# A matmul's moving operand read in four interleaved quarters instead of column by column

## The chip, the cores and the metric

The kernel runs on one core of one Trainium2 chip. The metric is device time in microseconds (us) for one execution of the program; times of single instructions are given in nanoseconds (ns). A core has TensorE (PE; PEld is its weight load), VectorE (DVE), ScalarE (ACT), GpSimd (POOL) and SyncE (SP), which run on their own and wait for each other by semaphores. SyncE, ScalarE and GpSimd issue the transfers (DMA).

## What is computed

The reference mixes two branches of the same input by a gate. Branch A is a Fourier mix written as four matrix products, branch B a dense layer with a squared ReLU and a second dense layer:

```python
# x: (1, 2048, 1024); dft_hid_*: (1024, 1024); dft_seq_*: (2048, 2048); w1: (1024, 3584); w2: (3584, 1024)
g = sigmoid((x * gate_w).sum(-1, keepdims=True))
a = einsum("bsd,ed->bse", x, dft_hid_re)
b = einsum("bsd,ed->bse", x, dft_hid_im)
y = einsum("ts,bse->bte", dft_seq_re, a) - einsum("ts,bse->bte", dft_seq_im, b)
h = einsum("bsd,df->bsf", x, w1) + b1
h = max(h, 0) ** 2
o = einsum("bsf,fd->bsd", h, w2) + b2
out = g * y + (1 - g) * o
```

All of it is float32.

## The kernel before

**Arithmetic.** Every product of two float32 blocks is made of three matmuls. Each operand is split into `hi` (the value rounded to the matmul's 32-bit type fp32r, ScalarE's `Copy`) and `lo` (the value minus `hi`, a VectorE subtraction), and `hi·hi`, `hi·lo` and `lo·hi` are added up in PSUM. Above that stand two levels of a seven-product scheme for 2x2 blocks (`FACTORS`, `SUMS_L`, `SUMS_R`, L59 to L72): seven products instead of eight, for sums and differences of blocks which VectorE makes (tiles named `sum`, or `raw` where a block is overwritten) or a transfer adds while it lands.

**Stages.** `x_stage` makes a and b of the hidden transform (tiles `ab`), `c_stage` the sequence transform (tiles `y`), two parts of `h_stage` the first dense layer (tiles `h`), and `o_stage` the second one and the mix (tiles `o`). Results between stages lie in DRAM.

**A step.** A block is 128 partitions x 2 x 512 values, 512 KB. A step is one pair of operands: `Group.run` (L534 to L560) issues for each of the up to four rows of 128 weight columns, for each of the two halves `kk`, and for each of the three pairs of `hi` and `lo` one matmul: weights of 128 x 128 (the stationary operand `a`) against 512 columns (the moving operand `b`). So a full step has 24 matmuls, and all 7896 of them have this shape, in any stage. The moving operand is a whole `hi` or `lo` tile, `b[:, kk, :]`: 512 neighbouring float32 of each partition. When a group of steps ends, VectorE or ScalarE takes the PSUM bank (`ps`) up: `ab<-u,ps` is such an addition.

**What each operand is in which stage.** In `x_stage` x is stationary and the transform's matrix (`w4`) is moving; in `c_stage` ab is stationary and the sequence matrix (`ct`) moving; in `h_stage` w1 is stationary and x moving; in `o_stage` w2 is stationary and h moving.

**Order.** The kernel's operations are recorded first (`Op`, `Queue`) and then put in order by `plan` (L1372 to L1521), a model of the machine with a cost per operation: TensorE's matmuls keep their order, each with a due time `MM` (0.2267 us) after the one before it; every other operation is due by the matmul that needs it, and each engine's queue takes what is ready and due first. `emit` (L1524) writes the result out, so an engine's instructions stand in the order that the model found. 55 `SLOTS` of one block each hold all operands; the four pairs of PSUM banks are given out in turn. Before the first step `WARM` = 44 small bf16 matmuls of 128 columns run on a tile of ones.

**Host side.** `kernel` (L1559) only re-lays the inputs with numpy (`laid`) and the output at the end.

Of the kernel before, what the change touches and what calls it, by code (L numbers as in the profile page):

```python
# [15 lines left out]
P = 128  # L16
S, D, F = 2048, 1024, 3584
# [18 lines left out]
MADE = {"T1": 2568, "T3": 11876}  # L36
TWICE_H = (1, 2, 5, 3, 4, 6, 7), (1, 2, 5, 3, 4, 6)

MM, MM_END, FIRST_MM = 0.2267, 0.18, 6.2
VEC, VEC_END, ACT, ACT_END = (0.07, 1.0417e-3), 0.39, (0.09, 0.843e-3, 0.04, 0.095), 0.41  # L40
ADDING = 0.85, 2.1, 2.2
ISSUE, RING, RATE, SEM, LANES = {"sync": 0.36, "scalar": 0.36, "gpsimd": 0.56}, {"sync": (1.8, 1.8), "scalar": (1.8, 1.8), "gpsimd": (1.6, 1.6)}, (420e3, 395e3), 0.06, 8
# [33 lines left out]
def gated_mix_kernel(ctx: ExitStack, tc: tile.TileContext, x4, xn, w4, ct, w1a, w1b, w2, b1, b2, gw, out):  # L76
# [143 lines left out]
    def run(*parts):  # L220

        for _ in zip_longest(*parts):
            pass
# [57 lines left out]
    class Part(Near):  # L281
# [21 lines left out]
        def load(self, engines):  # L303
            if self.lands:
                self.slots = [take("raw", width=self.width)]
                a, b = (b.at if isinstance(b, Kept) else b for b in self.blocks)
                at = self.slots[0][:, :, 0:self.width]
                next(engines).dma_start(at, a)
                nc.gpsimd.dma_start(at, b, accum_op=ADD)
            else:  # L310
                run(self.load_parts(engines))
# [24 lines left out]
        def sum(self):  # L336
            run(self.make_parts())
# [59 lines left out]
    class Operand:  # L397
# [28 lines left out]
        def sum(self):  # L426
            run(self.sum_parts())
# [86 lines left out]
    class Group:  # L514
# [27 lines left out]
        def run(self, st, mv, by_part=False):  # L542
            if not self.ps:
                self.prepare()
            self.at += 1
            ends = self.at % self.k == 0
            mms = [(r, kk, n) for r in range(self.rows) for kk in range(2) for n in range(3)]
            if by_part:
                mms.sort(key=lambda e: (e[1], e[0] // 2, e[2], e[0]) if e[1] == 0 else (e[1], e[2], e[0]))
            for r, kk, n in mms:  # L550
                a, b = ((st.hi, mv.hi), (st.hi, mv.lo), (st.lo, mv.hi))[n]
                nc.tensor.matmul(self.ps[r // self.per][:, r % self.per, :], a[:, kk, r * P:(r + 1) * P],
                                 b[:, kk, :], start=self.at == 1 and kk + n == 0 and not self.onto,
                                 stop=ends and kk == 1 and n == 2,
                                 skip_group_check=bool(self.at > self.k or self.onto))
                if ends and self.per == 1 and kk == 1 and n == 2:
                    self.done[0][0](r // 2, self.ps[r], r % 2)
                elif ends and (r % 2 or r == self.rows - 1) and kk == 1 and n == 2:
                    self.done[self.at // self.k - 1][0](r // 2, self.ps[r // 2])
            if self.at == self.k * len(self.done):  # L560
                banks.extend(self.pools)
# [1031 lines left out]
```

## Time and profile before

| what | value |
|---|---|
| median of 3 runs | 1817.81 us (1817.16 to 1818.1) |
| span of the profiled execution, first to last instruction | 1816.2 us |
| mean granted TensorE clock | 0.999 |
| instructions | 22349 |
| transfers | 562.63 MB, mean 310 GB/s |

The profile shows one execution. For it only the span is known; the times of the runs include what little lies around the span. A group's line gives the source line, engine, operation, the tiles written and read (`lo<-raw,hi` is the subtraction that makes `lo`), the shape and the count; behind the bar its busy time, the mean of one in ns, and the idle time of the engine before such instructions with what ended it. All operations are recorded by a helper and have its line, L1542, so that tiles tell them apart. A matmul's end is modelled, and consecutive matmuls overlap in the profile; their pace is read from start to start.

### The profile page before, as it was taken

The numbers are of one execution on the slowest core, as the hardware profiler recorded it, in microseconds if no ns is written. First come the engines' busy times: TensorE is split into PE (matmuls) and PEld (weight loads), VectorE is DVE, ScalarE is ACT, GpSimd is POOL, SyncE is SP. The second block draws the span as 40 slices with busy tenths as digits, with TensorE's granted clock in tenths as the row PEclk, the third lists the DMA queues.
The fourth block names the chain that finished last, engine by engine and source line by source line (L and its number), as shares of the span: only waits on it lengthen the run. The fifth ranks groups of instructions, "written<-read, shape, count | busy, mean of one in ns | idle before, by whom it ended". The sixth has DMA issues, their size and how long they took to land. (4 is left out here: it accounts for less than half of the span.)

```text
span 1816.2 us, 22349 instructions
## 1 busy us (share of the span) xinstructions
PE 1799.8 (99%) x7940; PEld 1484.5 (82%) x7940; DVE 1711.6 (94%) x1698; ACT 1157.5 (64%) x1274; POOL 284.2 (16%) x415
## 2 busy tenths in 40 slices
PE   9999999999999999999999999999999999999998
PEld 7888878888888888888878888788888888888886
DVE  8999989999999999999779999878998999999997
ACT  6465655774666664666583739967886567575662
POOL 1212112111211100111120201111121021101121
PEclk9999999999999999999999999999999999999999
DMA  9999999999998899989998889999999999979986
GB/s 376 322 393 380 384 331 302 323 273 292 261 354 264 227 306 383 311 216 351 314 371 278 279 299 329 375 381 327 345 362 253 335 241 303 328 192 349 316 218 149
DMA packets 158607, 562.63 MB, mean 310 GB/s; under 512 B 17808, under 2 KB 18080, under 8 KB 158496
## 3 DMA queue, kind: packets, MB, share of 16 engines
q1 hardware_dynamic: 98496, 351.99, 51.4%
q0 software_dynamic: 59712, 208.83, 43.1%
q8 instruction: 62, 1.02, 0.2%
q10 hardware_dynamic: 288, 0.39, 0.1%
q14 instruction: 49, 0.40, 0.1%
HBM read 402.28 MB, written 138.94 MB: 298 GB/s over the span
## 5 line engine op out<-in xcount | busy, mean ns | idle before, releaser
L1542 PE MATMUL ps<-hi 128*128 128x512 f32 x2188 | 852.2, 390 | 6.2 <-DVE h L1542 3.2
L1542 PE MATMUL ps<-hi,lo 128*128 128x512 f32 x2188 | 850.7, 389 | 1.0 <-DVE lo L1542 1.0
L1542 PE MATMUL ps<-lo,hi 128*128 128x512 f32 x2188 | 850.8, 389 | 0.6 <-DVE lo L1542 0.6
L1542 ACT ACTIVATE hi<-raw 128x1024 fp32r<-128x1024 f32 (+2 forms) x452 | 459.1, 1035 | 238.7 <-DVE raw L1542 76.1
L1542 PEld LDWEIGHTS ps<-hi 128*128 128x128 f32 x2188 | 410.6, 188 | 96.9 <-DVE h L1542 5.3
L1542 PEld LDWEIGHTS ps<-hi,lo 128*128 128x128 f32 x2188 | 410.7, 188 | 87.4 <-DVE lo L1542 1.8
L1542 PEld LDWEIGHTS ps<-lo,hi 128*128 128x128 f32 x2188 | 410.5, 188 | 86.4 <-DVE lo L1542 1.5
L1542 DVE TENSOR_TENSOR lo<-raw,hi 128x1024 fp32r<-128x1024 f32 (+2 forms) x385 | 451.5, 1190 | 29.1 <-ACT hi L1542 24.1
L1542 ACT ACTIVATE hi<-sum 128x1024 fp32r<-128x1024 f32 (+1 forms) x248 | 253.8, 1037 | 153.0 <-DVE sum L1542 103.3
L1542 DVE TENSOR_TENSOR lo<-sum,hi 128x1024 fp32r<-128x1024 f32 (+1 forms) x232 | 273.9, 1194 | 14.4 <-ACT hi L1542 5.4
L1542 PE MATMUL ps<-hi,both 128*128 128x512 f32 x888 | 285.0, 389 | 0.0
L1542 DVE TENSOR_TENSOR raw<-raw 128x1024 f32<-128x1024 f32 (+1 forms) x173 | 204.0, 1196 | 5.3 <-DMA raw<-in_w1a 2.6
L1542 PEld LDWEIGHTS ps<-hi,both 128*128 128x128 f32 x888 | 166.6, 188 | 34.7 <-DVE both L1542 0.2
L1542 DVE TENSOR_TENSOR sum<-raw 128x1024 f32<-128x1024 f32 (+2 forms) x180 | 175.6, 985 | 11.1 <-DMA raw<-in_w1a 2.3
L1542 PE MATMUL ps<-lo,both 128*128 128x512 f32 x444 | 172.7, 389 | 0.0
L1542 DVE TENSOR_TENSOR sum<-raw,sum 128x1024 f32<-128x1024 f32 (+2 forms) x135 | 141.3, 1049 | 2.3 <-DMA raw<-in_ct 1.4
L1542 ACT ACTIVATE u<-ps 128x1024 f32<-128x1024 f32 x104 | 101.2, 976 | 34.7 <-PE ps L1542 32.5
L1542 PEld LDWEIGHTS ps<-lo,both 128*128 128x128 f32 x444 | 83.4, 188 | 17.4
L1542 ACT ACTIVATE ps<-u 128x1024 f32<-128x1024 f32 x68 | 67.2, 989 | 35.5 <-DVE u L1542 16.3
L1542 DVE TENSOR_TENSOR u<-u,ps 128x1024 f32<-128x1024 f32 x74 | 86.8, 1184 | 1.9 <-PE ps L1542 1.0
L1542 ACT ACTIVATE both<-sum 128x512 fp32r<-128x512 f32 x74 | 46.3, 625 | 55.5 <-DVE sum L1542 49.2
L1542 DVE TENSOR_TENSOR h<-h,ps 128x1024 f32<-128x1024 f32 (+1 forms) x58 | 61.2, 1067 | 11.6 <-PE ps L1542 11.2
(82 smaller groups left out, 1002.2 us busy)
## 6 DMA issues: line engine op xcount, KB each, us to landing
raw<-in_ct SPq DMA_DIRECT2D x133, 512.0 KB, 8.9
raw<-h SPq DMA_DIRECT2D x104, 512.0 KB, 7.2
raw<-in_w SPq DMA_DIRECT2D x94, 512.0 KB, 9.0
raw<-copy SPq DMA_DIRECT2D x74, 512.0 KB, 7.1
raw<-ab SPq DMA_DIRECT2D x70, 512.0 KB, 10.0
raw<-in_x SPq DMA_DIRECT2D x51, 512.0 KB, 8.7
lo<-lo SPq DMA_DIRECT2D x50, 512.0 KB, 7.0
copy<-raw POOLq DMA_DIRECT2D x46, 512.0 KB, 9.3
```

What stands on the lines that cost most here:

```text
L1542: made = getattr(real[op.engine], op.name)(*(actual(a) for a in op.args), **{k: actual(v) for k, v in op.kwargs.items()})
```

## The change

The matmul's moving operand is read through another access pattern. `b[:, kk, :].rearrange("p (a b) -> p b a", a=4)` takes the 512 columns as 4 quarters of 128 and reads column 0 of each quarter, then column 1 of each quarter, and so on: 128 groups of four columns whose addresses lie 512 bytes apart. The result in PSUM is written in the order of reading, so its columns are permuted: column 4i + q of the result is column 128q + i of the operand. What follows from that is settled in numpy, before and after the program:

- `w4` is laid so that the permuted read of `x_stage` gives the natural order (its result is the stationary operand of the next stage);
- `ct` is laid permuted once, and the read permutes it again; h comes out of `h_stage` permuted once (x is laid as before there) and is permuted again when `o_stage` reads it, so that both branches' results have their columns in the order `twice`;
- the gate's input `xn` is laid in the order `twice`, and the output is put back at the end.

The planner's cost of a matmul is changed with it, from 0.2267 to 0.2157 us.

```diff
-MM, MM_END, FIRST_MM = 0.2267, 0.18, 6.2
+MM, MM_END, FIRST_MM = 0.2157, 0.18, 6.2
...
                 nc.tensor.matmul(self.ps[r // self.per][:, r % self.per, :], a[:, kk, r * P:(r + 1) * P],
-                                 b[:, kk, :], start=self.at == 1 and kk + n == 0 and not self.onto,
+                                 b[:, kk, :].rearrange("p (a b) -> p b a", a=4), start=self.at == 1 and kk + n == 0 and not self.onto,
...
+    seen = np.arange(512).reshape(4, 128).T.ravel()
+    twice = (512 * np.arange(4)[:, None] + seen[seen]).ravel()
     laid = {
...
-        "xn": x.reshape(P, 16, D).transpose(1, 0, 2),
-        "w4": np.stack([a.T.reshape(2, 2, 2, P, 2, 512).transpose(4, 0, 1, 3, 2, 5) for a in w]),
-        "ct": np.stack([a.T.reshape(8, 2, P, 2, 2, 512).transpose(3, 4, 0, 2, 1, 5) for a in c], axis=2),
+        "xn": x[twice].reshape(P, 16, D).transpose(1, 0, 2),
+        "w4": np.stack([a.T.reshape(2, 2, 2, P, 2, 512).transpose(4, 0, 1, 3, 2, 5) for a in w])[..., np.argsort(seen)],
+        "ct": np.stack([a.T.reshape(8, 2, P, 2, 2, 512).transpose(3, 4, 0, 2, 1, 5) for a in c], axis=2)[..., seen],
...
-    return np.ascontiguousarray(r.results[0]["out"].T).reshape(1, S, D)
+    return np.ascontiguousarray(r.results[0]["out"][:, np.argsort(twice)].T).reshape(1, S, D)
```

The number of instructions of each kind stays the same on every engine. TensorE's order stays as it was. The new planner's cost puts the other engines' instructions in another order from the first steps on; two places on VectorE show how. The first is in `x_stage`, where the additions out of PSUM `ab<-u,ps` begin (from 49.6 us on in the profile before). Before:

```order
L1542 TENSOR_TENSOR ab<-u,ps 128x1024
L1542 TENSOR_TENSOR lo<-sum,hi 128x1024
L1542 TENSOR_TENSOR sum<-raw,sum 128x1024
L1542 TENSOR_TENSOR ab<-u,ps 128x1024
L1542 TENSOR_TENSOR lo<-sum,hi 128x1024
L1542 TENSOR_TENSOR ab<-u,ps 128x1024
L1542 TENSOR_TENSOR lo<-sum,hi 128x1024
L1542 TENSOR_TENSOR ab<-u,ps 128x1024
L1542 TENSOR_TENSOR lo<-raw,hi 128x1024 x2
```

and with the change:

```order
L1542 TENSOR_TENSOR ab<-u,ps 128x1024
L1542 TENSOR_TENSOR lo<-sum,hi 128x1024
L1542 TENSOR_TENSOR sum<-raw,sum 128x1024
L1542 TENSOR_TENSOR ab<-u,ps 128x1024 x2
L1542 TENSOR_TENSOR lo<-sum,hi 128x1024 x2
L1542 TENSOR_TENSOR ab<-u,ps 128x1024
L1542 TENSOR_TENSOR lo<-raw,hi 128x1024
L1542 TENSOR_TENSOR ab<-u,ps 128x1024
L1542 TENSOR_TENSOR lo<-raw,hi 128x1024
```

The third and the fifth addition each stand one preparation (`lo`) earlier. The second place is in `o_stage`, where the additions `u<-u,ps` stand (at 1552.4 us in the profile before). Before:

```order
L1542 TENSOR_TENSOR sum<-raw,sum 128x512
L1542 TENSOR_TENSOR raw<-raw 128x1024 x2
L1542 TENSOR_TENSOR lo<-raw,hi 128x1024
L1542 TENSOR_TENSOR both<-sum,both 128x2x256
L1542 TENSOR_TENSOR lo<-raw,hi 128x1024 x3
L1542 TENSOR_TENSOR u<-u,ps 128x1024 x2
L1542 TENSOR_TENSOR u<-u 128x1024
L1542 TENSOR_TENSOR raw<-raw 128x1024
L1542 TENSOR_TENSOR u<-u,ps 128x1024
```

and with the change:

```order
L1542 TENSOR_TENSOR sum<-raw,sum 128x512
L1542 TENSOR_TENSOR raw<-raw 128x1024 x3
L1542 TENSOR_TENSOR u<-u,ps 128x1024 x2
L1542 TENSOR_TENSOR u<-u 128x1024
L1542 TENSOR_TENSOR lo<-raw,hi 128x1024
L1542 TENSOR_TENSOR u<-u,ps 128x1024
L1542 TENSOR_TENSOR u<-u 128x1024
L1542 TENSOR_TENSOR u<-u,ps 128x1024
L1542 TENSOR_TENSOR both<-sum,both 128x2x256
L1542 TENSOR_TENSOR lo<-raw,hi 128x1024 x2
```

Here two additions stand ahead of four `lo` subtractions and one `both` that came before them.

## The prediction

> **What bounds the kernel now.** I read the page's busy times first, then the stretches of 100 us, then TensorE alone from its first wide matmul to its last, then the chain of waits and TensorE's own waits, and last the timeline of single matmuls. The page's head gives each engine's busy time:
>
> ```profile
> span 1816.2 us, 22349 instructions
> PE 1799.8 (99%) x7940; PEld 1484.5 (82%) x7940; DVE 1711.6 (94%) x1698; ACT 1157.5 (64%) x1274; POOL 284.2 (16%) x415
> ```
>
> TensorE is occupied all the time, VectorE 94% of it, ScalarE 64%. The columns of the next view are the stretch in us and its length, then the busy us of PE, PEld, DVE, ACT and POOL with their counts, the granted clock, the DMA share and GB/s.
>
> ```profile
> 0.00:100.00 100.00, 97.60 (x450) 79.94 (x451) 93.20 (x86) 57.76 (x60) 20.52 (x39) 1.00 0.98 355
> 100.00:200.00 100.00, 99.88 (x441) 82.40 (x440) 99.81 (x105) 57.22 (x59) 18.04 (x34) 1.00 1.00 390
> 200.00:300.00 100.00, 98.67 (x436) 81.33 (x435) 92.58 (x87) 55.63 (x58) 24.18 (x38) 1.00 0.97 322
> 300.00:400.00 100.00, 99.37 (x438) 81.78 (x437) 95.31 (x102) 72.43 (x82) 13.01 (x16) 1.00 1.00 303
> 400.00:500.00 100.00, 100.00 (x443) 82.81 (x442) 99.42 (x99) 55.32 (x60) 18.52 (x22) 1.00 1.00 282
> 500.00:600.00 100.00, 100.00 (x443) 82.81 (x442) 96.22 (x92) 62.81 (x67) 16.22 (x25) 1.00 0.93 309
> 600.00:700.00 100.00, 100.00 (x443) 82.81 (x442) 99.64 (x98) 60.62 (x65) 5.08 (x6) 1.00 0.89 290
> 700.00:800.00 100.00, 100.00 (x443) 82.81 (x442) 96.06 (x97) 59.29 (x64) 18.29 (x22) 1.00 1.02 309
> 800.00:900.00 100.00, 98.98 (x436) 81.10 (x435) 91.83 (x85) 65.09 (x68) 10.50 (x15) 1.00 0.89 294
> 900.00:1000.00 100.00, 98.64 (x435) 81.34 (x434) 83.89 (x73) 60.38 (x67) 16.46 (x29) 1.00 0.92 331
> 1000.00:1100.00 100.00, 100.00 (x443) 82.78 (x442) 98.61 (x88) 58.47 (x67) 14.72 (x25) 1.00 0.85 293
> 1100.00:1200.00 100.00, 98.61 (x433) 80.69 (x432) 86.63 (x97) 97.21 (x125) 10.21 (x18) 1.00 0.99 360
> 1200.00:1300.00 100.00, 99.69 (x438) 81.63 (x437) 86.77 (x102) 72.18 (x91) 21.05 (x34) 1.00 1.00 353
> 1300.00:1400.00 100.00, 99.62 (x440) 82.17 (x439) 91.83 (x97) 76.38 (x90) 17.10 (x26) 1.00 1.00 317
> 1400.00:1500.00 100.00, 100.00 (x443) 82.79 (x442) 99.35 (x103) 57.14 (x63) 14.01 (x15) 1.00 0.96 277
> 1500.00:1600.00 100.00, 100.00 (x443) 82.81 (x442) 99.72 (x98) 69.31 (x73) 17.07 (x25) 1.00 0.98 306
> 1600.00:1700.00 100.00, 100.00 (x442) 82.80 (x442) 99.58 (x100) 63.98 (x69) 9.07 (x9) 1.00 0.91 283
> 1700.00:1800.00 100.00, 100.00 (x443) 82.79 (x442) 92.95 (x95) 55.71 (x61) 17.05 (x18) 1.00 0.86 230
> 1800.00:1816.00 16.00, 8.75 (x39) 6.93 (x37) 8.24 (x11) 0.60 (x1) 3.14 (x3) 0.93 0.64 131
> ```
>
> Two things are to be seen. TensorE does 433 to 443 matmuls in every full stretch behind the first, whatever VectorE, ScalarE and the transfers do beside it, at a granted clock of 1.00. And VectorE is near its own limit in places: 99.4 to 99.8 of 100 us in six of these stretches, and ScalarE 97.2 in one. The next rows are TensorE alone from the first wide matmul to the last, the chain that ended last, and TensorE's two largest waits for another engine (us in total, times, longest):
>
> ```profile
> 5.80:1808.40 1802.60, 1795.04 (x7896) 1.00 0.95 311
> PE ps L1542 27%; DVE o L1542 0%; DVE lo L1542 0%; DVE h L1542 0%; DVE both L1542 0%; DVE sum L1542 0%
> PE ps L1542 <- DVE h L1542: 3.2, 4, 1.4
> PE ps L1542 <- DVE lo L1542: 1.6, 2, 1.0
> ```
>
> So 7896 wide matmuls take 1802.6 us, 228.3 ns each with all waits in; the chain is one unbroken run of matmuls over its last 27% of the span; and what TensorE waits for is small (3.2 us in four waits is the largest entry). The pace of the matmul sets the time. In the timeline of the middle (start us, duration us) the first and the last of 28 matmuls in a row are
>
> ```profile
> 899.74 0.39 PE L1542 MATMUL ps<-hi 128*128 128x512 f32 x1
> 905.86 0.39 PE L1542 MATMUL ps<-hi 128*128 128x512 f32 x1
> ```
>
> which is 6.12 us for 27 steps: 226.7 ns from start to start. The 0.39 us is a modelled end and overlaps the next. 7896 x 226.7 ns is 1790.0 us; the other 26 us of the span are 5.8 before the first wide matmul, 7.8 after the last, and 12.6 of waits.
>
> **The change, part by part.** The reading order alone touches the chip's work per instruction: 7896 matmuls stay 7896, with the same 512 columns and the same weights. The trace has no strided read of a moving operand, so its price has to be bounded. What is there are the warm-up matmuls of 128 bf16 columns, 33 at the slow start and 8 after the clock has risen:
>
> ```profile
> 1.06 3.70 PE L1542 MATMUL ps<-ones 128*128 128x128 bf16 x33 [1.06 <-DVE ones L1542]
> 4.87 0.61 PE L1542 MATMUL ps<-ones 128*128 128x128 bf16 x8
> L1542 PE MATMUL ps<-ones x44: 219/311/311, 1.1 to 5.3; 128*128 128x128 bf16 x44
> ```
>
> The third row has a single one's modelled duration, 311 ns slow and 219 ns fast. Slow: (3.70 - 0.31) / 32 steps = 106 ns. Fast: (0.61 - 0.22) / 7 = 56 ns. Half of 106 is 53, so at the fast clock 53 ns go with the columns and 3 ns with the instruction. For 512 columns that makes 4 x 53 + 3 = 215, and 216 with the roundings: 10.7 ns less than the 226.7 that the wide matmul takes. This excess is the same beside busy and idle neighbours (443 matmuls in each full stretch), so it belongs to the instruction: to its 4-byte columns, read one after the other.
>
> Bounds per matmul, then: below, 216, the excess gone, 7896 x 10.7 ns = 84.5 us off; at nothing, 226.7; above, the slow pace of the first warm-up matmuls, 4 x 106 = 424 ns, if each column had to wait a second turn because the next lies 512 bytes further on, 7896 x 197 ns = 1556 us on top. I take 216. Its row is the nearest (same engine, same clock, only the element size differs), and reading four quarters in turn is a change of just that in which the wide matmul differs from it. The trace doesn't prove the cause, so the other ends stay as rivals.
>
> [...]
>
> What is hidden beneath the matmul stays hidden. The weight loads:
>
> ```profile
> L1542 PEld LDWEIGHTS ps<-hi 128*128 128x128 f32 x2188 | 410.6, 188 | 96.9 <-DVE h L1542 5.3 <-DVE u L1542 2.3 <-DVE ab L1542 2.0
> ```
>
> 188 ns each fit under 216. The host's layouts cost nothing: the same blocks of 512 KB are moved, their columns in another order. The planner's constant changes only the order of DVE, ACT, SP and POOL; each keeps its operations. In the two places shown, additions out of PSUM come ahead of preparations, by one to four places: at 1.13 us each (two `lo` end to end last 2.35, one lasts 1.22, in the rows at 1493 us below), a preparation is up to 4.5 us later. I cost this at nothing, since TensorE waited for a `lo` only twice, 1.6 us in all, so operands lie ready before their turn; without that lead it is up to 4.5 us at such a place.
>
> ```profile
> 1492.31 1.22 DVE L1542 TENSOR_TENSOR o<-ps,o 128x1024 f32<-128x1024 f32 x1
> 1493.45 2.35 DVE L1542 TENSOR_TENSOR lo<-raw,hi 128x1024 fp32r<-128x1024 f32 x2
> ```
>
> What is late next is VectorE. TensorE alone would end at 1816.2 - 84.5 = 1731.7 us, and VectorE has 1711.6 us of work. If a stretch could borrow nothing from its neighbours, each would last as long as its busiest engine: TensorE needs 95.3 (100 x 216 / 226.7), VectorE what its column shows. Seven stretches (0, 200, 800, 900, 1200, 1300 and 1700) last 95.3: 667. Ten are held by VectorE: 99.8 + 95.3 + 99.4 + 96.2 + 99.6 + 96.1 + 98.6 + 99.4 + 99.7 + 99.6 = 983.7. One is held by ScalarE: 97.2. The last 16.2 us hold 39 matmuls, so 0.4 us go and 15.8 stay. Together 1764 us. Borrowing (work done ahead into the 55 slots) would bring it towards 1732; new waits of VectorE for its own operands, which it now makes up for in its 6% of idle time, push it up. I let the two cancel and take 1764 for the span.
>
> The transfers are the other neighbour:
>
> ```profile
> q1 hardware_dynamic: 98496, 351.99, 51.4%
> q0 software_dynamic: 59712, 208.83, 43.1%
> ```
>
> Together 94.5% of the span, 1716 us. If that share were rigid, the stretches with a share above 0.953 would end by it, and the sum grows by 2.7 + 0.2 + 1.7 + 4.7 + 0.6 + 3.9 + 1.8 + 4.7 + 4.7 = 25 us, to 1789. I don't charge it: at the same share of 1.00 the stretches move 282, 303, 317, 353 and 390 GB/s, so a packet's time holds waiting that can shrink. It is the upper end of this case.
>
> The profiled span of 1816.2 lies 1.6 under the median of the runs, 1817.81; with that added the forecast is 1765.6, so 1765, and its own range 1733 to 1791.
>
> **The rivals.** First, that only part of the excess goes. If what the fast warm-up matmul has per column holds for any column (56 / 128 = 0.4375 ns), 512 columns take 224 and the reading order saves 2.7 ns: 21 us, and VectorE's full stretches (99.4 to 99.8 of 98.8) give some 4 back: 1801 us. For it speaks that the split of 56 into 53 and 3 hangs on a rounded number; against it, that 106 / 2 leaves some fixed part in any case.
>
> Second, that the order of reading does nothing, because the 10.7 ns are paid once per fp32 matmul, say with its weight load. Then TensorE stays at 226.7, and the planner's orders are made for a pace that doesn't come: additions earlier, preparations up to 4.5 us later, one or two waits of that size. 1816 to 1822. The trace cannot exclude it, as every wide matmul has the same shape.
>
> Third, the other side: the scattered read is slower. Its place is each of the 7896 matmuls, its price up to 197 ns each, 1818 + 1556 = 3374 us, by the bound above. It decides early: 0.2% of this kernel, about what a measurement of it can tell from no change, is 3.6 us, which 0.46 ns more per matmul makes. For it speaks that successive columns never lie side by side any more; against it, that each of the four places is read on in order, so the neighbouring words are used four columns later.
> [...]
>
> **How the numbers follow.** The forecast, matmuls near 216 ns with VectorE next in line, 0.62. The partial gain 0.10. No change of the pace 0.12, of which 0.02 come out faster, 0.06 within 0.2% and 0.04 slower. The slower read 0.16. Faster by over 0.2%: 0.62 + 0.10 + 0.02 = 0.74; same 0.06; slower 0.04 + 0.16 = 0.20. The range runs from 1733, where nothing but TensorE counts, to 1822, the end of the case without a new pace; it leaves out the slower read and some 0.04 beside the other cases' ends.
>
> **What would show it.** Right: single matmuls of the timeline 216 ns apart; about 460 in a full stretch of 100 us; VectorE above 96% of the span; TensorE's waits for DVE `lo`, `sum` or `u` grown from under 4 us to some 30. Wrong: 226.7 ns between matmuls as before (second rival), 224 (first), or above 227 (third). If the pace is 216 and the time 1735, VectorE's full stretches were work done early and not need; if it is 216 and the time above 1790, the transfers or the order hold it.

## The result, and the profile after

| | before | with the change |
|---|---|---|
| median of 4 runs each | 1817.49 us (1816.81 to 1818.1) | 2247.84 us (2232.36 to 2260.22) |
| ratio, with its 95% interval | | 1.2364 (1.2312 to 1.2416) |
| span of the profiled execution | 1816.2 us | 2230.6 us |

The kernel is slower by 24%. The page's head of the changed kernel:

```profile
span 2230.6 us, 22340 instructions
PE 2216.2 (99%) x7940; PEld 1508.9 (68%) x7940; DVE 1728.3 (77%) x1698; ACT 1158.5 (52%) x1274; POOL 284.4 (13%) x415
```

TensorE is as full as before, while VectorE fell from 94% to 77% of the span with nearly the same work in microseconds. Whatever grew lies in TensorE itself. TensorE alone from its first wide matmul to its last, and its two largest waits for another engine's tiles (us in total, times, longest):

```profile
6.00:2223.00 2217.00, 2211.73 (x7896) 1.00 0.80 253
```

```profile
PE ps L1542 <- DVE lo L1542: 4.3, 2, 2.6
PE ps L1542 <- ACT hi L1542: 1.2, 2, 1.0
```

The same 7896 matmuls take 2217.0 us where they took 1802.6, at the same granted clock of 1.00, with waits as small as before: 414.4 us more, and the span grew by 2230.6 - 1816.2 = 414.4 us. It is the pace of the matmul that grew, 280.8 ns on average instead of 228.3. In the timeline around 900 us, the first and the last of 26 matmuls in a row:

```profile
899.63 0.45 PE L1542 MATMUL ps<-hi 128*128 128x512 f32 x1
...
906.72 0.45 PE L1542 MATMUL ps<-lo,hi 128*128 128x512 f32 x1
```

That is 7.09 us for 25 steps, 283.6 ns; over all such steps of the execution the mean is 283.3. The stretches of 100 us (columns as in the prediction) show a second pace:

```profile
200.00:300.00 100.00, 100.00 (x367) 69.41 (x366) 77.84 (x68) 47.74 (x49) 15.44 (x25) 1.00 0.88 301
600.00:700.00 100.00, 100.00 (x355) 67.44 (x354) 74.85 (x69) 50.16 (x51) 10.77 (x18) 1.00 0.70 237
```

A matmul that reaches into the stretch is counted too, so a pace is 100 us over one less than the count: 273 ns in the first stretch and 282 in the second. VectorE, ScalarE and the transfers all have idle time in both.

### The profile page after: what moved, and what is told of

The parts are those of the page before. It is cut to its first block, busy times and chain, and to the rows that moved or that the text cites. A ratio compares the mean times of both kernels' runs of the same rounds, so it can differ in the third digit from the quotient of the medians.

```text
span 2230.6 us, 22340 instructions
## 1 busy us (share of the span) xinstructions
PE 2216.2 (99%) x7940; PEld 1508.9 (68%) x7940; DVE 1728.3 (77%) x1698; ACT 1158.5 (52%) x1274; POOL 284.4 (13%) x415
## 2 busy tenths in 40 slices
DMA packets 158608, 562.63 MB, mean 252 GB/s; under 512 B 17809, under 2 KB 18081, under 8 KB 158497
## 4 chain that ended last, share of the span: by engine, by line
PE 99%; DVE 0%; issue 0%; DMA 0%; ACT 0%; DVEq 0%; ACTq 0%
PE ps L1542 99%; DVE lo L1542 0%; DMA raw<-in_x 0%; ACT hi L1542 0%; DVE sum L1542 0%; DVE o L1542 0%; DVE both L1542 0%; DVE raw L1542 0%; DVEq L1542 0%; ACTq L1542 0%
## 5 line engine op out<-in xcount | busy, mean ns | idle before, releaser
L1542 PE MATMUL ps<-lo,hi 128*128 128x512 f32 x2188 | 972.5, 445 | 2.6 <-DVE lo L1542 2.6
L1542 PE MATMUL ps<-hi,lo 128*128 128x512 f32 x2188 | 972.4, 445 | 1.7 <-DVE lo L1542 1.7
L1542 PE MATMUL ps<-hi 128*128 128x512 f32 x2188 | 972.4, 445 | 1.2 <-ACT hi L1542 1.2
L1542 PEld LDWEIGHTS ps<-hi,lo 128*128 128x128 f32 x2188 | 417.4, 191 | 198.2 <-DVE lo L1542 3.4
L1542 PEld LDWEIGHTS ps<-lo,hi 128*128 128x128 f32 x2188 | 417.3, 191 | 198.0 <-DVE lo L1542 3.3
L1542 PEld LDWEIGHTS ps<-hi 128*128 128x128 f32 x2188 | 417.2, 191 | 197.3 <-ACT hi L1542 2.2
L1542 PE MATMUL ps<-hi,both 128*128 128x512 f32 x888 | 332.8, 444 | 0.7 <-DVE both L1542 0.7
L1542 PE MATMUL ps<-lo,both 128*128 128x512 f32 x444 | 197.1, 444 | 0.0
L1542 DVE TENSOR_TENSOR h<-h,ps 128x1024 f32<-128x1024 f32 (+1 forms) x58 | 62.1, 1072 | 57.3 <-PE ps L1542 56.6
L1542 DVE TENSOR_TENSOR both<-sum,both 128x512 fp32r<-128x512 f32 x74 | 50.9, 687 | 29.3 <-ACT both L1542 29.2
```

The costliest lines, as they stand in the source:

```text
L1542: made = getattr(real[op.engine], op.name)(*(actual(a) for a in op.args), **{k: actual(v) for k, v in op.kwargs.items()})
```

## The experiments

All kernels differ from the change in the reading order, in the planner's constant `MM`, or in both; with each reading order, numpy's layouts follow. A matmul's pace is read from its starts. `order_only`, `read_only` and `g2_plan` ran four times each, and their median is given; every other kernel ran once.

**Read or order?** The change has two parts, and each was run alone. The planner's constant alone (`order_only`):

```diff
+MM, MM_END, FIRST_MM = 0.2157, 0.18, 6.2
+                                 b[:, kk, :], start=self.at == 1 and kk + n == 0 and not self.onto,
```

> The planner's constant alone: contiguous read as before, orders planned for 215.7 ns. If the change's loss lies in the read alone: 226.7 ns between matmuls and 1816 to 1822 us, new waits of at most a few us. If the orders have a part in it: clearly above 1822 us.

Measured: 1856.58 us, ratio 1.0206 (1.019 to 1.0221), with matmuls 227 ns apart as before. TensorE's largest waits:

```profile
PE ps L1542 <- DMA lo<-raw: 11.2, 1, 11.2
PE ps L1542 <- DVE lo L1542: 10.2, 11, 1.8
PE ps L1542 <- ACT hi L1542: 5.0, 3, 3.2
PE ps L1542 <- DMA lo<-sum: 4.1, 1, 4.1
```

The orders cost 38 us by themselves (1856.58 against 1818.18 for the kernel before beside it) where TensorE keeps its old pace, far more than the few us that were expected. Not all of it is waiting: at its longer waits the granted clock fell to 0.50, for 3 to 14 us at a time (its mean is 0.97 from 300 to 400 us and 0.76 from 1700 to 1720), and some 45 matmuls there start 427 ns apart instead of 227, which is 9 of the 38 us. The largest single wait is for a transfer of GpSimd's queue that completes a `lo` by adding. It stands behind four stores to `out`:

```profile
1683.90 1.19 POOL L1542 DMA_DIRECT2D out<-o  x1 [17.88 <-DVE o L1542]
...
1695.45 1.19 POOL L1542 DMA_DIRECT2D out<-o  x1 [4.92 <-DVE raw L1542]
1699.29 0.90 POOL L1542 DMA_DIRECT2D lo<-raw  x1 [2.65 <-ACT hi L1542]
...
1717.94 0.79 PE L1542 MATMUL ps<-lo,hi 128*128 128x512 f32 x1 [11.18 <-DMA lo<-raw]
```

It was issued at 1699.3 us, and the matmul that needs it began at 1717.9, where such a transfer lands after 8.7 us in the median. In the kernel before, GpSimd issues it ahead of the four stores:

```profile
1658.09 0.84 POOL L1542 DMA_DIRECT2D lo<-raw  x1 [28.56 <-ACT lo L1542]
...
1672.27 3.66 POOL L1542 DMA_DIRECT2D out<-o  x3 [6.34 <-DVE raw L1542]
1687.90 1.18 POOL L1542 DMA_DIRECT2D out<-o  x1 [11.97 <-DVE sum L1542]
```

That the stores held it up is read from the queue's order and was not tried by itself. The read alone (`read_only`):

```diff
+MM, MM_END, FIRST_MM = 0.2267, 0.18, 6.2
+                                 b[:, kk, :].rearrange("p (a b) -> p b a", a=4), start=self.at == 1 and kk + n == 0 and not self.onto,
```

> The read in four quarters alone, planner's constant as before. If the loss lies in the read alone: 273 to 283 ns between matmuls and 2180 to 2260 us, the same as the change. If the orders have a part in it: nearer to 1817 us than the change.

Measured: 2252.47 us, ratio 1.2384 (1.2363 to 1.2405), with matmuls 283 ns apart. The read carries the whole loss. The 38 us of the orders don't show in the change: at this slower pace the other engines have room (VectorE is busy for 77% of the span, not 94%), and beyond the matmuls' pace the starts hold some 8 us in the change and under 1 us in `read_only`.

**What in the read?** The surcharge of 283 over 226.7 ns, 56.6 ns, is one column's time (226.7 / 512 = 0.44 ns) for each of the 128 groups of four, but also a quarter of a column's time for each of the 512 columns that lie in another place than the one before. Four orders were to tell such readings apart; all keep the planner's 0.2267. `g2` reads two halves in turn, 256 groups of two; `g128` reads four groups of 128 columns that lie 16 bytes apart; `lines` and `pairs` read four and two neighbouring columns of each quarter in turn, in 128 groups of four and 256 of two. A line, in labels and expectations, is a name for four neighbouring columns of the operand.

```diff
+b[:, kk, :].rearrange("p (a b) -> p b a", a=2)             # g2
+b[:, kk, :].rearrange("p (a b) -> p b a", a=128)           # g128
+b[:, kk, :].rearrange("p (a b c) -> p b a c", a=4, c=4)    # lines
+b[:, kk, :].rearrange("p (a b c) -> p b a c", a=4, c=2)    # pairs
```

> The read of the change with two halves instead of four quarters (256 groups of two columns, 1024 bytes apart), planner's constant as before. The change's matmuls were mostly 283 ns from start to start, 56.6 more than 226.7, which is 0.44 ns, one column time (226.7 / 512), for each of its 128 groups. Theory W (each return of the inner loop costs one column time): 226.7 x (512 + 256) / 512 = 340 ns, about 2710 us in all. [...] Theory D (the 512-byte distance costs): 283 ns or more.

> [...] Planner's constant as before. Theory W: 226.7 x 516 / 512 = 228.5 ns, about 1830 us. [...] Theory D: 226.7 ns, as before.

> [...] Planner's constant as before. Theory W: as the change, 283 ns, about 2250 us. [...] Theory D: one far jump in four columns, 226.7 + 56.6 / 4 = 241 ns, about 1930 us.

> [...] Planner's constant as before. Theory W: 340 ns, about 2710 us, far slower than the change. [...] Theory D: 255 ns.

Measured: 1803.63, 3655.78, 2131.99 and 3513.73 us, beside 1820.49 for the kernel before on this chip. With two halves, the first and the last of 34 matmuls in a row in the timeline are

```profile
899.72 0.38 PE L1542 MATMUL ps<-lo,hi 128*128 128x512 f32 x1
...
906.84 0.38 PE L1542 MATMUL ps<-lo,hi 128*128 128x512 f32 x1
```

7.12 us for 33 steps: 215.8 ns. That is the pace of the forecast, and no theory had it. The other three, in the stretch from 600 to 700 us (length, TensorE's busy us and count, clock, DMA share, GB/s), one fence each for `g128`, `lines` and `pairs`:

```profile
600.00:700.00 100.00, 100.00 (x218) 1.00 0.50 147
```

```profile
600.00:700.00 100.00, 100.00 (x374) 1.00 0.80 255
```

```profile
600.00:700.00 100.00, 100.00 (x227) 1.00 0.52 140
```

Read from single starts these are 461, 268 and 443 ns. Theory W falls with `g2` (216, not 340) and `g128` (461, not 228.5). A quarter of a column's time for each column that lies in another place falls with `g2`, where all of them do and the matmul (216) is faster than the contiguous one, and with `pairs`, where half of them do and it takes 443. Theory D falls with `g128`, 16 bytes apart and slow.

**Number of places or distance?** Two places at the change's distance, then at 16 bytes; four places at another distance; eight and 32 places:

```diff
+b[:, kk, :].rearrange("p (h a b) -> p h b a", h=2, a=2)    # two_512
+b[:, kk, :].rearrange("p (h a b) -> p h b a", h=64, a=2)   # two_16
+b[:, kk, :].rearrange("p (h a b) -> p h b a", h=2, a=4)    # four_256
+b[:, kk, :].rearrange("p (a b) -> p b a", a=8)             # g8
+b[:, kk, :].rearrange("p (a b) -> p b a", a=32)            # g32
```

> Two alternating places as in the halves (216 ns), but 512 bytes apart as in the change (273 to 283 ns): the first kilobyte in two halves, then the second. Planner's constant as before. Theory S (the number of places read in turn decides, four are too many): 216 ns, about 1803 us. Theory D (places 512 bytes apart get in each other's way, places 1024 bytes apart don't): 270 ns or more, above 2150 us.

> Two places in turn, 16 bytes apart, in pieces of eight columns: line 0 and line 1 alternate, then line 2 and line 3; planner's constant as before. [...] With a cost of nearness (what 128 places 16 bytes apart would then owe their 461 ns to): above 226.7 ns.

> Four places in turn as in the change, but 256 bytes apart, first in one kilobyte of the block, then in the other. Planner's constant as before. If the number of places decides: 273 to 283 ns, 2180 to 2260 us. If the distance of 512 bytes has a part in it: another pace.

> Eight places in turn, 256 bytes apart; planner's constant as before. Theory S (the more places are read in turn, the more each column costs: two 216 ns, four 283, 128 places 461): clearly above 283 ns, 330 or more, above 2600 us. [...]

> 32 places in turn, 64 bytes apart; planner's constant as before. Theory S: near the 461 ns of 128 places, about 3650 us. [...]

Measured: 1806.93, 1806.82, 2252.76, 3855.85 and 3434.79 us; the kernel before took 1816.6 to 1818.2 beside them. Two places are at 216 ns at either distance, and four places 256 bytes apart are at the 283 ns of those 512 bytes apart. In the stretch from 600 to 700 us, `four_256`, `g8` and `g32`:

```profile
600.00:700.00 100.00, 100.00 (x354) 1.00 0.73 241
```

```profile
600.00:700.00 100.00, 100.00 (x206) 1.00 0.48 149
```

```profile
600.00:700.00 100.00, 100.00 (x232) 1.00 0.62 160
```

By single starts 283, 487 and 433 ns. With two and with four places the number counts (216 against 283) and the distance, 16 to 1024 bytes, doesn't. But eight places are slower than 32 (487 against 433), which theory S doesn't have.

**How many neighbours in a row?** The even columns first, so that successive columns lie 8 bytes apart; two neighbouring columns, and four, from two halves; runs of sixteen columns from four quarters:

```diff
+b[:, kk, :].rearrange("p (a b) -> p b a", a=256)           # g256
+b[:, kk, :].rearrange("p (a b c) -> p b a c", a=2, c=2)    # duos
+b[:, kk, :].rearrange("p (a b c) -> p b a c", a=2, c=4)    # lines2
+b[:, kk, :].rearrange("p (a b c) -> p b a c", a=4, c=16)   # runs16
```

> [...] Planner's constant as before. [...] Theory S: as a contiguous read, 226.7 ns.

> Two neighbouring columns of the first half, then two of the second, and so on; 256 innermost groups of two as in the kernel with two columns of each quarter (443 ns), but with two places. Planner's constant as before. [...] Theory J (jumps inside a group's neighbourhood cost whatever the number of places): 443 ns, 3510 us.

> Whole lines of four columns, alternately from the two halves; 128 jumps as with whole lines of four quarters (269 ns), but two places. Planner's constant as before. If each jump costs 0.33 ns ((269 - 226.7) / 128): 269 ns, 2130 us. If more than two places cost: 226.7 ns or less, about 1817 us.

> Sixteen neighbouring columns (64 bytes) of each quarter in turn, 32 jumps per matmul. Planner's constant as before. If a jump between places costs 0.33 ns: 226.7 + 32 x 0.33 = 237 ns, about 1900 us. [...]

Measured: 3575.37, 2698.57, 1990.94 and 1850.17 us; the kernel before took 1816.6 and 1816.7 beside them. Matmuls are 451, 340, 250 and 231 ns apart (`lines2` alternates between 246 and 254, the steps of `runs16` are 235, 227 and 232 in turn). `g256` and `duos` in the stretch from 600 to 700 us:

```profile
600.00:700.00 100.00, 100.00 (x223) 1.00 0.49 137
```

```profile
600.00:700.00 100.00, 100.00 (x296) 1.00 0.71 189
```

Theory J falls with `duos`, at 340 where it has 443. `lines2` lies between its two cases (250 between 227 and 269), and `runs16` between the contiguous read and the 237 of its expectation (231), which says that places and jumps both have a part. And `g256`, which reads every second column in the order of the addresses and has no far jump but one, is among the slowest (451).

Two more orders vary the even columns and the contiguous read: `evens2` reads the even columns of the two halves alternately and then the odd ones, and `swap` reads each four neighbouring columns in the order 0, 2, 1, 3.

```diff
+b[:, kk, :].rearrange("p (a b c) -> p c b a", a=2, c=2)    # evens2
+b[:, kk, :].rearrange("p (b a c) -> p b c a", a=2, c=2)    # swap
```

> The even columns of the two halves alternately, then the odd ones. [...] Planner's constant as before. [...]

> Line after line as in a contiguous read, but within each line in the order 0, 2, 1, 3. Planner's constant as before. [...] If the contiguous read is fast because it has unit steps: above 270 ns, as every other order with 128 or more short groups and no long run.

Measured: 1819.02 and 1817.03 us, beside 1817.35 for the kernel before. In the stretch from 600 to 700 us, `evens2` and `swap`:

```profile
600.00:700.00 100.00, 99.48 (x439) 1.00 0.89 293
```

```profile
600.00:700.00 100.00, 99.97 (x441) 1.00 0.88 294
```

Both have the 227 ns of the contiguous read. `evens2` and `g256` both read the even columns before the odd ones; with the two halves by turns the matmul takes 227 ns, without 451. And the contiguous read has no privilege of its own: in `swap` only every fourth step goes to the next column, at the same pace. All orders by their pace:

| reading order | the columns in the order of reading | ns from start to start |
|---|---|---|
| two places in turn, 1024, 512 or 16 bytes apart (`g2`, `two_512`, `two_16`) | 0, 256, 1, 257; 0, 128, 1, 129; 0, 4, 1, 5 | 216 |
| contiguous; `swap`; `evens2` | 0, 1, 2, 3; 0, 2, 1, 3; 0, 256, 2, 258 | 227 |
| sixteen neighbours of four places, four of two, four of four (`runs16`, `lines2`, `lines`) | a jump after each 16, 4, 4 | 231, 250, 268 |
| four places in turn (the change, `four_256`) | 0, 128, 256, 384, 1; 0, 64, 128, 192, 1 | 273 to 283 |
| two neighbours of two places (`duos`) | 0, 1, 256, 257, 2, 3 | 340 |
| two neighbours of four places; even columns; 32, 128, 8 places | 0, 1, 128, 129; 0, 2, 4, 6; 0, 16, 32; 0, 4, 8; 0, 64, 128 | 443, 451, 433, 461, 487 |

The table tells what each order costs. Why one is faster than another, and why eight places are slower than 32 and 128, no run shows.

**The halves with their planner's constant.** This is the fastest version measured (`g2_plan`):

```diff
+MM, MM_END, FIRST_MM = 0.2157, 0.18, 6.2
+                                 b[:, kk, :].rearrange("p (a b) -> p b a", a=2), start=self.at == 1 and kk + n == 0 and not self.onto,
```

> The change with two halves in place of four quarters, planner's constant 0.2157 as in the change. The halves with the old planner's constant gave 216 ns between matmuls and 1803.6 us, with 84 us of waits of TensorE (27 of them for ScalarE's ps). If these waits come from VectorE and ScalarE being near their limits, as the forecast's 1764 us had it, the new order brings it to 1755 to 1785 us. If they come from the order planned for a slower TensorE alone: 1735 to 1750 us. If the orders don't matter: 1800 us.

Measured: 1797.74 us, ratio 0.9886 (0.9869 to 0.9903) to the kernel before. TensorE's largest waits, and two of its stretches:

```profile
PE ps L1542 <- DVE lo L1542: 19.5, 17, 2.1
PE ps L1542 <- DMA lo<-raw: 12.4, 1, 12.4
PE ps L1542 <- DMA lo<-sum: 7.1, 4, 4.3
```

```profile
1400.00:1500.00 100.00, 91.22 (x404) 77.39 (x403) 95.75 (x99) 53.93 (x59) 14.25 (x15) 0.97 0.93 279
...
1600.00:1700.00 100.00, 86.18 (x384) 73.64 (x383) 90.87 (x89) 53.59 (x57) 10.86 (x11) 0.93 0.89 280
```

The starts of its matmuls hold some 81 us over 216 ns each, where the kernel before has 12.6 over 226.7. So of the 84.5 us that the pace gives, about 69 were lost again. Some 11 us of the 81 are 51 matmuls that start 427 ns apart where the granted clock had fallen to 0.50 at a wait (hence the 0.97 and 0.93 in the rows); the rest is nearly all waiting. Where most was lost, between 1600 and 1700 us, VectorE was busy for 90.9 us: there TensorE waited 12.4 us for the same transfer as in `order_only`, again behind four stores, not for a full VectorE.

Of the three expectations the last one, that the orders don't matter, comes nearest. The halves with the old orders (`g2`) took 1803.6 us, on another chip, and their starts hold 84 us over the pace, so the new orders gave little. What they did is to change what TensorE waits for. The largest entry of `g2` is ScalarE's taking up of PSUM banks, which has 0.5 us with the new orders:

```profile
PE ps L1542 <- ACT ps L1542: 27.1, 15, 3.5
```

## Why the prediction was wrong

**What bounds the kernel** was right: it is the matmul's pace, and all 414.4 us came through it.

**The step that failed** is the choice of 216 ns for the read in four quarters: "I take 216. Its row is the nearest". The runs show 273 to 283 ns in its place. The bounds around it, 216 and 424, held these. The first half of the step, that 10.7 ns of the contiguous matmul are owed to how its columns are read and can be had, is shown: two places in turn reach 215.8. The second half, that reading four quarters in turn has them too, is wrong: four places cost 46 to 57 ns more than the contiguous read. The row chosen was near in engine and clock (granted 1.00 in both), though more than the element size differed (it has 128 columns, not 512), and the 56 ns of the warm-up matmul are those of a contiguous read as well; no row of the trace had a second place in it, so no row was near in the thing that was changed. Why four places cost more, no run shows. The 53 and 3 ns in the sum that gave 216, and the clock that rises in the warm-up, are estimates from its two paces, 106 and 56 ns: the profile has a granted clock of 1.00 at both. One of 0.50 was seen at other places only, where 512 columns took 427 ns, four times the 106.

**The third rival** was the right one in its place and sign, and its price was a bound: 52.5 ns on average of at most 197. Its point of decision, 0.46 ns per matmul, was passed a hundredfold. It had 0.16. The argument against it, that each place is read on in order and its neighbouring words are used a few columns later, fits two places (216 ns, back two columns later) and not four (273 to 283 ns).

**The second rival's price** was too small. Orders planned for a pace that doesn't come cost 38 us, not one or two waits of up to 4.5 us. Those 4.5 us were misread too: in the second place shown, `both` and the `lo` behind it stand seven instructions later, not four, about 8 us at 1.13 each. Above all I costed the moves on VectorE that I had looked at, and not GpSimd's queue, where an adding transfer was planned behind stores, nor the half clock at the waits.

**VectorE next in line** could be tested with the halves. At 216 ns the kernel takes 1797.7 us and not 1765. The pace's share of the sum was right; the neighbours' was 33 us too small. VectorE's waits are there, 27 us with `lo`, `h`, `both` and `u`, near the 30 that I gave as their sign. Beside them stand 19.5 us for transfers, which I had kept out of the sum and put at the upper end of that case, 1791, and the 11 us at the half clock, for which the sum had no term.

**The host's layouts** show no cost, as said: the change moved 562.63 MB as before. The weight loads at 188 to 191 ns stayed hidden.

## What to carry to other kernels

A reading order of an operand that no row of the trace has is a new instruction for the profile: the bounds may be honest and the middle is a guess, so measure the pace of one such matmul first, which one profile shows to a nanosecond. Where one reordering pays, its neighbours need not: two places in turn gained 5% of the matmul (216 ns for 226.7), four lost 20 to 25% (273 to 283), eight more than doubled it (487). And a faster bottleneck is worth only what the engines and queues next to it can follow (here about 69 of 84.5 us were lost again); an order planned for another pace costs by itself (here 38 us).

## What the runs showed of the hardware beside it

The changed kernel has two paces, 273 and 283 ns, with the same instructions. In the profiled execution they change only where TensorE had waited, and stay until the next such place: 273 from about 21 us, 283 from 566 us on (after a wait that ends in the row below), 273 again from 1828 us and 283 from 2067 us.

```profile
565.22 0.54 PE L1542 MATMUL ps<-hi,lo 128*128 128x512 f32 x1 [1.73 <-DVE lo L1542]
...
565.87 0.45 PE L1542 MATMUL ps<-lo,hi 128*128 128x512 f32 x1
566.15 0.45 PE L1542 MATMUL ps<-hi,lo 128*128 128x512 f32 x1
```

Such changes of pace would explain why its runs spread over 28 us and those of the kernel before over 1.3, but only one run of the change was profiled. In it 2823 steps were at 273 ns; at 283 they would have taken 28 us more, which makes 2261 us beside the slowest run's 2260. What the two paces come from stays open; from 15 us on `read_only` was at 283 ns throughout, and `four_256` but for seven steps, of which six had no wait before them. Another stretch of the change's profiled execution had a granted clock of 0.50, and there matmuls started 427 ns apart, four times the 106 ns of the slow warm-up matmul of 128 columns:

```profile
380.00:382.00 2.00, 2.00 (x7) 0.50 0.65 168
```

```profile
380.25 0.63 PE L1542 MATMUL ps<-hi,lo 128*128 128x512 f32 x1
...
382.39 0.63 PE L1542 MATMUL ps<-lo,hi 128*128 128x512 f32 x1
```

2.14 us for five steps is 428 ns: at half the clock the read in four quarters shows no surcharge that these rows could tell. The contiguous read (`order_only`) and the halves (`g2_plan`) have 427 ns in such stretches as well, so there the reading order made no difference.
